# Block sums formed in PSUM, q weighted on GpSimd, and the last stores paired over two queues

## The chip, the core and the metric

The kernel runs on one core of a Trainium2 chip. Its engines work side by side: TensorE (PE in the profile; PEld is its weight load) multiplies matrices into the eight banks of PSUM, VectorE (DVE) and ScalarE (ACT) do elementwise work and read PSUM, GpSimd (POOL) does elementwise work in SBUF and issues loads, SyncE (SP) issues transfers. An engine runs its instructions in the order in which they were written, and waits on semaphores for the others. The metric is the device time of one execution in microseconds (us), as the median of several runs.

## The reference

Linear attention with cosine weights, followed by a gated feed-forward layer (SwiGLU). Cut to what is computed:

```python
# q, k, v: (8 batches, 8 heads, 576 positions, 64)
theta = np.pi / 2.0 * pos / S
def phi(x):                       # relu, then two weighted halves
    r = np.maximum(x, 0.0)
    return np.concatenate([r * cos(theta), r * sin(theta)], axis=-1)
q_p, k_p = phi(q), phi(k)
kv  = np.einsum('bhsf,bhsd->bhfd', k_p, v)
z   = np.sum(k_p, axis=2)
num = np.einsum('bhsf,bhfd->bhsd', q_p, kv)
den = np.einsum('bhsf,bhf->bhs', q_p, z)[..., None] + 1e-06
x   = (num / den).transpose(0, 2, 1, 3).reshape(4608, 512)
g   = x @ w_gate                  # 512 x 1536
out = (g / (1 + exp(-g)) * (x @ w_val)) @ w_out     # 1536 x 512
```

## The kernel before, in words

The 4608 tokens are cut into nine groups (tg 0 to 8) of 512 tokens, four tiles of 128 each. A group first runs twelve feed-forward steps (fc 0 to 11, `ffn_mm` L531): four matmuls with w_gate and four with w_val, each 512 columns wide; ACT takes silu of the first bank (L537), DVE multiplies it with the second into `ht` (L542). Then the group's output is made from `ht` and w_out.

For groups 0 and 1 that is done tile by tile (`ffn_out`, L580). For groups 2 to 8 `out_by_quarters` (L618) treats the product `ht` times w_out as a product of 2x2 blocks and computes it with seven block products in place of eight, each 12 matmuls of 256 columns (L640). The operands that this needs are sums of blocks: T1 to T4 of w_out are made once; S1 to S4 of `ht` are made in each group by DVE (`token_sum`, L611), the last parts of them behind the last feed-forward step (`sums_behind`). The products go, in this order, into PSUM banks: a (first product), e (S3 T3), b (S2 T2), a again (added to the first: this is C11), b again (S1 T1 added), c (A22 T4), b again (S4 B22 added). Each quarter C11, C12, C21, C22 of the output lies in an SBUF tile `ob`; every intermediate sum is made there. ACT copies bank a into C12 (L653); DVE's `added` (L647) then adds a bank, scaled by DOWN, to another quarter, five times a group: C22 = e + C12, C21 = b + C22, C22 = b + C22, C21 = c + C21, C12 = b + C12. ACT writes C11 (L663). A product that adds into b has to wait until DVE has read what stood there.

Attention is threaded between those steps. `at(slot, f)` puts a function into a plan, and `slot(n)` calls what is planned for step n of the whole program; a group has 16 slots, 12 for its feed-forward steps and four in `out_by_quarters` (`slot_of(0)` to `slot_of(3)`). For batch b of 2 to 7 there: POOL waits, by a tiny copy `hold2` (`load_behind`, L840), until the turned q of batch b-1 has landed, and then loads q, k and v of batch b (L107; k and v of batch 3 elsewhere). ACT takes relu of a quarter of q in place (L234) and DVE multiplies it with a table into `r_q` (`phi_q`, L251), four times a batch, in slots 11 to 14 of group b-2 for batches 4 and up. SP turns `r_q` by two DMA transposes into `phit` (L274) at the end of that group. k is treated by ACT and v by DVE (`vmul`, L255), and in the next group TensorE forms k times v (L301). `a_tile2` (L415) makes one tile of attention output, DVE divides it (L425, L434, L438) into `x`, and SP turns it by a DMA transpose into `xT` (L515) for the next group. SP also issues the stores of `ob` (L570), all in the order in which they are written.

`rel`, the pool of `r_q`, has one buffer; `raw`, that of q, k and v as loaded, three; `ob` two. PSUM banks are handed out by `take`, which picks the bank that has been unused for longest and avoids those held under a name (a, b, c, e above).

The profile calls each piece by the line of its instruction, or of the helper that issues it.

Of the kernel before, what the change touches and what calls it, by code (L numbers as in the profile page):

```python
# [11 lines left out]
BF16 = mybir.dt.bfloat16  # L12
FP16 = mybir.dt.float16
AF = mybir.ActivationFunctionType
ALU = mybir.AluOpType
# [3 lines left out]
def kernel(  # L19
# [10 lines left out]
    nc = tc.nc  # L30
    B, H, S, D = q.shape
    P = 128
    G = H // 2
    J = G // 2
    SH = 64
    NC = S // SH
    d_model, d_ff = moe_w_gate.shape
# [8 lines left out]
    UP = float(2 ** 12)  # L46
    DOWN = 1.0 / UP
    HC = FC // 2
    HT = T // 2
    HD = d_model // 2  # L50
# [3 lines left out]
    rel = ctx.enter_context(tc.tile_pool(name="rel", bufs=1))  # L54
# [13 lines left out]
    now = [0]  # L68
    held = {}

    def take(n, hold=None):

        taken = {x for r in held.values() for x in r}
        free = [b for b in range(0, 8, n) if not any(b <= x < b + n for x in taken)]

        b0 = min(free, key=lambda b: (n == 1 and hold is not None and hold[0] == "o" and b ^ 1 not in taken,
                                      sorted(used[b:b + n], reverse=True)))
        if hold is not None:
            held[hold] = range(b0, b0 + n)
        touch(range(b0, b0 + n))  # L80
        return banks[:, b0] if n == 1 else banks[:, b0:b0 + n]

    def touch(r):
        now[0] += 1
        for x in r:
            used[x] = now[0]
# [5 lines left out]
    raws = {}  # L92
# [102 lines left out]
    csk, cst = cs_all[:, 0], cs_all[:, 1]  # L195
# [49 lines left out]
    def phi_q(b, g):  # L245

        if g == 0:
            st[b, "q"] = rel.tile([P, G, NC, 2, D], BF16, name="r_q")
        o = raws[b, "q"][:, g]
        relu_op("act", o, o)  # L250
        nc.vector.tensor_tensor(out=st[b, "q"][:, g], in0=o.unsqueeze(2).to_broadcast([P, NC, 2, D]),  # L251
                                in1=tab, op=ALU.mult)

    def vmul(b, g):
        nc.vector.tensor_tensor(  # L255
# [262 lines left out]
    def ffn_mm(tg, fc, lo=0, hi=GH, which=(0, 1)):  # L518

        n = (hi - lo) * SH  # L520
        ts = slice(lo // 2, hi // 2)
        fs = slice(fc * P, (fc + 1) * P)
        if 0 in which:
            if 2 * n <= 512:
                both = take(1, ("f", tg, fc, lo))
                st["f", tg, fc, lo] = [both[:, 0:n], both[:, n:2 * n]]
            else:
                st["f", tg, fc, lo] = [take(1)[:, 0:n] for _ in range(2)]
        for i in which:
            for kc in range(KC):  # L530
                nc.tensor.matmul(out=st["f", tg, fc, lo][i], lhsT=(wg_sb, wv_sb)[i][:, kc, fs], rhs=xT[tg][:, ts, kc],  # L531
                                 start=(kc == 0), stop=(kc == KC - 1))
# [34 lines left out]
    def store(t, cols=slice(0, d_model), queues=None):  # L567
        for e in range(2):
            idx = 2 * t + e
            (queues or (nc.sync, nc.sync))[e].dma_start(out=out_v[idx // NC, idx % NC][:, cols],  # L570
                                                        in_=ob_of(t)[e * SH:(e + 1) * SH, cols])

    def ffn_out(t, f0=0, f1=None):

        f1 = FC if f1 is None else f1
        if f0 == 0:
            o_ps[t] = take(1, ("o", t))
        r = t % OUT * P
        for fc in range(f0, f1):
            nc.tensor.matmul(out=o_ps[t], lhsT=ht[:, fc, r:r + P], rhs=wo_sb[:, fc],  # L580
                             start=(fc == 0), stop=(fc == FC - 1))
        if f1 < FC:
            return
        ps = o_ps.pop(t)
        give_back(("o", t))
        if t % 2 == 0:
            nc.scalar.mul(out=ob_of(t), in_=ps, mul=DOWN)
        else:
            nc.vector.tensor_single_scalar(out=ob_of(t), in_=ps, scalar=DOWN, op=ALU.mult)
        store(t)  # L590
# [21 lines left out]

    def sums_behind(fc):
        for n, lo, hi in {7: ((3, 0, 4),), 8: ((1, 0, 4),), 9: ((2, 0, 4),), 10: ((4, 0, 4), (3, 4, 6)),
                          11: ((1, 4, 6), (2, 4, 6), (4, 4, 6))}.get(fc, ()):
            token_sum(n, lo, hi)

    def out_by_quarters(tg, slot_of):  # L618

        last = tg == NTG - 1  # L620
        t0 = tg * OUT
        for t in (t0, t0 + 2):
            ob_of(t)
        C11, C12 = (obs[t0 // 2][:, :, x * HD:(x + 1) * HD] for x in range(2))
        C21, C22 = (obs[t0 // 2 + 1][:, :, x * HD:(x + 1) * HD] for x in range(2))

        def home(nm, parts=1):
            return [take(1, ("o", tg, nm, i)).rearrange("p (t x) -> p t x", x=HD) for i in range(parts)]

        def free(nm, parts=1):  # L630
            for i in range(parts):
                give_back(("o", tg, nm, i))

        def at_of(x, i):
            return x[i][:, 0] if len(x) == 2 else x[0][:, i]

        def product(to, a, b, first):
            for i in range(2):
                for kc in range(HC):
                    nc.tensor.matmul(out=at_of(to, i), lhsT=a[:, kc, i * P:(i + 1) * P], rhs=b[:, kc],  # L640
                                     start=first and kc == 0 and (i == 0 or len(to) == 2),
                                     stop=kc == HC - 1, skip_group_check=True)

        def added(o, ps, x):
            for i in range(len(ps)):
                sl = slice(i, i + 1) if len(ps) == 2 else slice(0, 2)
                nc.vector.scalar_tensor_tensor(out=o[:, sl], in0=ps[i][:, 0:1] if len(ps) == 2 else ps[i],  # L647
                                               scalar=DOWN, in1=x[:, sl], op0=ALU.mult, op1=ALU.add)

        nb = 2 if last else 1  # L650
        a = home("a")
        product(a, aq[:, 0, 0], bq[:, 0, 0], True)
        nc.scalar.mul(out=C12, in_=a[0], mul=DOWN)  # L653
        e = home("e")
        product(e, S3, T3, True)
        added(C22, e, C12)
        b = home("b", nb)
        free("e")
        slot_of(0)
        product(b, S2, T2, True)  # L660
        added(C21, b, C22)
        product(a, aq[:, 1, 0], bq[:, 1, 0], False)
        nc.scalar.mul(out=C11, in_=a[0], mul=DOWN)  # L663
        free("a")
        if last:
            for t in (t0, t0 + 1):
                store(t, slice(0, HD))
        slot_of(1)
        product(b, S1, T1, False)
        added(C22, b, C22)  # L670
        if last:
            for t in (t0 + 2, t0 + 3):
                store(t, slice(HD, d_model))
        c = home("c")
        product(c, aq[:, 1, 1], T4, True)
        added(C21, c, C21)
        free("c")
        for t in (t0 + 2, t0 + 3):
            store(t, slice(0, HD) if last else slice(0, d_model))
        slot_of(2)  # L680
        product(b, S4, bq[:, 1, 1], False)
        added(C12, b, C12)
        free("b", nb)
        for t in (t0, t0 + 1):
            store(t, slice(HD, d_model) if last else slice(0, d_model), (nc.sync, nc.scalar) if last else None)
        slot_of(3)


# [149 lines left out]
    def load_behind(b):  # L838

        nc.gpsimd.tensor_copy(out=hold2, in_=phit[b - 1][0:1, :, 0, 0, 0])  # L840
        load(b, "q")
        if b > 3:
            load_kv(b)

    def load_kv(b):
        for nm in ("k", "v"):
            load(b, nm)
# [7 lines left out]
    for b in range(2, B):  # L855
        s0 = SLOTS * (b - 1)
        keng = "dve" if b == 2 else "act"
        steps = [lambda b=b, g=g: phi_q(b, g) for g in range(G)]
        steps += [lambda b=b, g=g: (relu_k(b, g, g + 1, keng), vmul(b, g)) for g in range(G)]
        if b == 2:  # L860
            fs, tq = [s0 + i for i in (0, 0, 1, 1, 4, 5, 5, 6)], (s0 + 2, s0 + 2)
        else:
            p0 = s0 - SLOTS
            fs, tq = [p0 + 11 + i for i in range(8)], (p0 + 15, p0 + 16)
            if b == 3:
                fs, tq = [p0 + 12 + i for i in range(4)] + [s0 + 4, s0 + 4, s0 + 5, s0 + 5], (s0 + 2, s0 + 2)
            at(p0 + 3 if b < 5 else p0 + 1, lambda b=b: load_behind(b))
        tk = (s0 + 4, s0 + {2: 8, 3: 7}.get(b, 5))
        for s, f in zip(fs, steps):
            at(s, f)  # L870
        for e in range(2):
            at(tq[e], lambda b=b, e=e: qturn_dma(b, e))
        at(tk[-1], lambda b=b: kv_mm(b), lambda b=b: kv_out2(b))
        at(tk[-1] + 1, lambda b=b: kv_free(b))
# [59 lines left out]
```

## Time and profile before

| what | us |
|---|---|
| median of 8 runs (323.44 to 324.16) | 323.8 |
| the profiled execution itself | 323.11 |
| its span, first to last instruction | 321.0 |
| DVE busy in it | 225.0 |
| POOL busy in it | 35.3 |
| the seven-product stretch of group 7 (274.06 to 283.1) | 9.04 |
| the same stretch of group 2 (110.9 to 121.04) | 10.14 |

Times of single instructions come from one execution, the one of 323.11 us. In a row of a timeline the first number is the start in us from the beginning of the span, the second the length; an `x` with a number counts instructions that were merged. In brackets stands how long the engine sat idle before it, and what it waited for. TensorE's ends are modelled, and spans on POOL are rough. Groups follow each other at about 32.8 us: group 2 begins at 87.8, group 3 at 121.3, group 4 at 154.1, group 5 at 187.0, group 6 at 219.9, group 7 at 252.3 and group 8 at 283.2.

### The profile page before, as it was taken

Reading aid. Unit: us, or ns where it says so; the run is one execution under the profiler, and the core shown is the slowest. Engines: PE = TensorE matmul, PEld = TensorE weight load, DVE = VectorE, ACT = ScalarE, POOL = GpSimd, SP = SyncE. Lnnn points to the kernel's source line nnn. Section 1 sums busy time; section 2 is a strip of 40 time slices with the busy share of each in tenths; the row PEclk is TensorE's granted clock in tenths of the full one; section 3 lists DMA queues with packets and bytes.
Section 4 is the critical chain, followed back from the end, with each engine's and each line's share of the span. In section 5 each row is a group of like instructions: output and inputs, shape, how many; then the busy total and the mean of one; then the engine's idle time right before and its main releaser. Section 6 shows DMA issues by size and latency. Waiting matters only on the chain.

```text
span 321.0 us, 6625 instructions
## 1 busy us (share of the span) xinstructions
PE 308.9 (96%) x2624; PEld 182.8 (57%) x2624; DVE 225.0 (70%) x448; ACT 130.1 (41%) x237; POOL 35.3 (11%) x60
## 2 busy tenths in 40 slices
PE   8899999999999989999999999999999999999990
PEld 4596555454445575558554855476547644854580
DVE  7873876788658888598859875988487448643750
ACT  7553556662436345334433543244431132223210
POOL 6755102010100200020002000300000000000000
PEclk9999999999999999999999999999999999999997
DMA  7999999988996987999696969597941411150014
GB/s 260 216 199 197 205 203 142 217 112 109 175 196 89 162 110 153 128 144 146 141 136 87 205 133 131 76 184 158 139 67 33 99 34 34 35 130 3 0 27 104
DMA packets 74862, 41.06 MB, mean 128 GB/s; under 512 B 50000, under 2 KB 69968, under 8 KB 74832
## 3 DMA queue, kind: packets, MB, share of 16 engines
q1 hardware_dynamic: 52480, 22.95, 40.1%
q0 software_dynamic: 22192, 17.57, 36.5%
q8 instruction: 20, 0.33, 0.4%
q10 hardware_dynamic: 160, 0.13, 0.2%
q14 instruction: 10, 0.08, 0.1%
HBM read 37.75 MB, written 9.44 MB: 147 GB/s over the span
## 4 chain that ended last, share of the span: by engine, by line
PE 76%; DVE 10%; DMA 5%; issue 3%; SPq 2%; ACT 2%; DVEq 0%; POOLq 0%; POOL 0%; ACTq 0%
PE banks L531 49%; PE banks L640 14%; PE banks L580 6%; DMA phit<-r_q 3%; PE banks L301 2%; DMA raw_q<-in_q_dram 2%; DVE ht L542 2%; DVE ob L647 2%; DVE sums L611 2%; PE banks L415 1%; SPq L274 1%; DVE r_q L251 1%; PE banks L461 1%; PE banks L397 1%; SPq L570 1%
## 5 line engine op out<-in xcount | busy, mean ns | idle before, releaser
L537 ACT ACTIVATE sg<-banks 128x512 bf16<-128x512 f32 (+2 forms) x116 | 65.8, 568 | 120.2 <-PE banks L531 113.2
L531 PE MATMUL banks<-xT,wv_sb 128*128 128x512 bf16 (+2 forms) x464 | 111.3, 364 | 0.0
L531 PE MATMUL banks<-xT,wg_sb 128*128 128x512 bf16 (+2 forms) x464 | 111.3, 364 | 0.0
L542 DVE TENSOR_TENSOR ht<-sg,banks 128x512 f16<-128x512 bf16 (+2 forms) x116 | 74.5, 648 | 51.5 <-PE banks L531 44.5
L531 PEld LDWEIGHTS <-wv_sb 128*128 128x128 bf16 x464 | 44.9, 98 | 48.7
L531 PEld LDWEIGHTS <-wg_sb 128*128 128x128 bf16 x464 | 43.2, 98 | 41.5
L640 PEld LDWEIGHTS <-ht 128*128 128x128 f16 x336 | 32.4, 98 | 6.8 <-issue 2.9
L647 DVE SCALAR_TENSOR_TENSOR ob<-banks,ob 128x512 f32<-128x512 f32 (+1 forms) x38 | 24.6, 647 | 13.7 <-PE banks L640 13.5
L640 PEld LDWEIGHTS <-sums 128*128 128x128 f16 x252 | 24.6, 98 | 2.9
L255 DVE TENSOR_TENSOR v<-raw_v,tab 128x1152 bf16<-128x1152 bf16 x31 | 22.7, 752 | 0.2 <-ACT raw_v L691 0.2
L580 PE MATMUL banks<-wo_sb,ht 128*128 128x512 f16 x96 | 22.7, 379 | 0.0
L438 DVE TENSOR_TENSOR x<-banks,rec 128x512 bf16<-128x512 f32 (+1 forms) x32 | 21.6, 675 | 1.3 <-PE banks L397 0.3
L640 PE MATMUL banks<-wt_sb,ht 128*128 128x256 f16 x168 | 19.5, 272 | 2.2 <-DVE ob L647 2.2
L251 DVE TENSOR_TENSOR r_q<-raw_q,tab 128x1152 bf16<-128x1152 bf16 x24 | 17.9, 752 | 5.2 <-ACT raw_q L234 5.1
L640 PE MATMUL banks<-wo_sb,ht 128*128 128x256 f16 x168 | 20.6, 273 | 0.0
L640 PE MATMUL banks<-wt_sb,sums 128*128 128x256 f16 x168 | 19.5, 273 | 0.0
L234 ACT ACTIVATE raw_k<-raw_k 128x576 bf16<-128x576 bf16 (+1 forms) x25 | 17.0, 694 | 0.0
L234 ACT ACTIVATE raw_q<-raw_q 128x576 bf16<-128x576 bf16 x24 | 15.4, 675 | 2.9 <-DMA raw_q<-in_q_dram 2.9
L611 DVE TENSOR_TENSOR sums<-ht 128x1024 f16<-128x1024 f16 (+1 forms) x28 | 15.5, 553 | 0.2
L840 POOL COPY hold<-phit 1x2 bf16<-1x2 bf16 x5 | 0.9, 175 | 132.2 <-DMA phit<-r_q 132.2
L580 PEld LDWEIGHTS <-ht 128*128 128x128 f16 x96 | 9.1, 98 | 8.9 <-issue 0.2
L415 PEld LDWEIGHTS <-phit 128*128 128x128 bf16 (+1 forms) x240 | 10.0, 100 | 6.5 <-issue 1.3
(95 smaller groups left out, 210.4 us busy)
## 6 DMA issues: line engine op xcount, KB each, us to landing
out_dram<-ob SPq DMA_DIRECT2D x64, 128.0 KB, 2.4
raw_k<-in_k_dram POOLq DMA_DIRECT2D x7, 576.0 KB, 8.8
raw_q<-in_q_dram POOLq DMA_DIRECT2D x6, 576.0 KB, 6.5
raw_v<-in_v_dram POOLq DMA_DIRECT2D x6, 576.0 KB, 11.6
wo_sb<-in_moe_w_out_dram POOLq DMA_DIRECT2D x3, 512.0 KB, 13.1
wg_sb<-in_moe_w_gate_dram POOLq DMA_DIRECT2D x5, 256.0 KB, 8.9
wv_sb<-in_moe_w_val_dram POOLq DMA_DIRECT2D x5, 256.0 KB, 9.2
wo_sb<-in_v_dram SPq DMA_DIRECT2D x2, 576.0 KB, 4.1
```

The source lines that it names most:

```text
L234: nc.scalar.activation(out=out, in_=in_, func=AF.Relu)
L251: nc.vector.tensor_tensor(out=st[b, "q"][:, g], in0=o.unsqueeze(2).to_broadcast([P, NC, 2, D]), in1=tab, op=ALU.mult)
L255: nc.vector.tensor_tensor(out=v2s[b % 2][:, g, :, :, 0:D], in0=(first if b == 0 and g == 0 else {"v": raw_of(b, "v")})["v"][:, g].unsqueez ...
L415: nc.tensor.matmul(out=ps[ms, e, g * D1:(g + 1) * D1], lhsT=phit[b][:, e, g, c:c + n].rearrange("p c s -> p (c s)"), rhs=kv2s[b % 2][:, e, ...
L438: nc.vector.tensor_tensor(out=st["x", t].rearrange("p (y e d) -> p e y d", e=2, d=D)[:, :, ys], in0=ps[:, :, 0:2 * J * D1].rearrange("p e ...
L531: nc.tensor.matmul(out=st["f", tg, fc, lo][i], lhsT=(wg_sb, wv_sb)[i][:, kc, fs], rhs=xT[tg][:, ts, kc], start=(kc == 0), stop=(kc == KC - 1))
L537: nc.scalar.activation(out=sg[:, 0:n], in_=st["f", tg, fc, lo][0], func=AF.Silu, scale=DOWN)
L542: nc.vector.tensor_tensor(out=ht[:, fc, r:r + n], in0=st.pop(("s", tg, fc, lo))[:, 0:n], in1=ps[1], op=ALU.mult)
L580: nc.tensor.matmul(out=o_ps[t], lhsT=ht[:, fc, r:r + P], rhs=wo_sb[:, fc], start=(fc == 0), stop=(fc == FC - 1))
L611: nc.vector.tensor_tensor(out=o[:, lo:hi], in0=x[:, lo:hi], in1=y[:, lo:hi], op=op)
L640: nc.tensor.matmul(out=at_of(to, i), lhsT=a[:, kc, i * P:(i + 1) * P], rhs=b[:, kc], start=first and kc == 0 and (i == 0 or len(to) == 2), ...
L647: nc.vector.scalar_tensor_tensor(out=o[:, sl], in0=ps[i][:, 0:1] if len(ps) == 2 else ps[i], scalar=DOWN, in1=x[:, sl], op0=ALU.mult, op1= ...
```

## The change

Three things are done at once.

`out_by_quarters` forms sums in PSUM. ACT copies bank a into bank b before the third product, which then adds to it. DVE adds the scaled C22, which ACT has written from e, to bank b, and puts the result into bank c; the sixth product adds to that. C21 and C12 become plain scaled copies, of bank c by ACT and of bank b by DVE. The bank manager `take` learns which banks were last filled whole by matmuls (`filled`), so that a bank which another engine writes first (`seeded`) is one of these. Four banks are held at once now, a, b, e and c.

The part S4(4,6) of the sums is made after DVE's reading of bank b, and no longer in `sums_behind`. For batches 4 to 7 `phi_q` on ACT and DVE is replaced by `phi_q_whole` on POOL: 18 operations of 128x256, called right behind that batch's loads. Batches 2 and 3 keep `phi_q`.

In the last group, C11, C22 and C21 are each stored by two transfers of two tiles (`store_two`), one on SP and one on ACT, in place of four on SP. C12 is stored as before.

```diff
-    def take(n, hold=None):
+    filled = [False] * 8
+
+    def take(n, hold=None, fills=False, seeded=False):
 
         taken = {x for r in held.values() for x in r}
-        free = [b for b in range(0, 8, n) if not any(b <= x < b + n for x in taken)]
+        free = [b for b in range(0, 8, n) if not any(b <= x < b + n for x in taken)
+                and (filled[b] or not seeded)]
...
+        filled[b0:b0 + n] = [fills or seeded] * n
...
+    def phi_q_whole(b):
+        r_q = st[b, "q"] = rel.tile([P, G, NC, 2, D], BF16, name="r_q")
+        for c in range(NC):
+            for w in range(2):
+                nc.gpsimd.tensor_scalar(out=r_q[:, :, c, w], in0=raws[b, "q"][:, :, c], scalar1=0.0,
+                                        scalar2=csk[:, c, w:w + 1], op0=ALU.max, op1=ALU.mult)
...
+    def store_two(t, cols):
+        for e in range(2):
+            (b, c), (b1, _) = divmod(2 * t + e, NC), divmod(2 * t + 2 + e, NC)
+            assert b == b1
+            (nc.sync, nc.scalar)[e].dma_start(
+                out=out_v[b, c:c + 3:2, :, cols].rearrange("c p f -> p c f"),
+                in_=obs[t // 2][e * SH:(e + 1) * SH, :, cols])
...
         for n, lo, hi in {7: ((3, 0, 4),), 8: ((1, 0, 4),), 9: ((2, 0, 4),), 10: ((4, 0, 4), (3, 4, 6)),
-                          11: ((1, 4, 6), (2, 4, 6), (4, 4, 6))}.get(fc, ()):
+                          11: ((1, 4, 6), (2, 4, 6))}.get(fc, ()):
...
+        def copied(eng, o, ps, x=DOWN):
+            for p_, o_ in each(ps, o):
+                if eng == "act":
+                    nc.scalar.mul(out=o_, in_=p_, mul=x)
+                else:
+                    nc.vector.tensor_single_scalar(out=o_, in_=p_, scalar=x, op=ALU.mult)
...
-        a = home("a")
+        a = home("a", fills=True)
         product(a, aq[:, 0, 0], bq[:, 0, 0], True)
-        nc.scalar.mul(out=C12, in_=a[0], mul=DOWN)
-        e = home("e")
+        b = home("b", nb, seeded=True)
+        for p_, o_ in each(b, a[0]):
+            nc.scalar.copy(out=p_, in_=o_)
+        e = home("e", fills=True)
         product(e, S3, T3, True)
-        added(C22, e, C12)
-        b = home("b", nb)
+        nc.scalar.mul(out=C22, in_=e[0], mul=DOWN)
+        c = home("c", seeded=True)
         free("e")
+        product(b, S2, T2, False)
+        for p_, o_, x_ in each(b, c[0], C22):
+            nc.vector.scalar_tensor_tensor(out=o_, in0=x_, scalar=UP, in1=p_, op0=ALU.mult, op1=ALU.add)
+        token_sum(4, 4, 6)
         slot_of(0)
-        product(b, S2, T2, True)
-        added(C21, b, C22)
         product(a, aq[:, 1, 0], bq[:, 1, 0], False)
-        nc.scalar.mul(out=C11, in_=a[0], mul=DOWN)
+        copied("act", C11, a)
         free("a")
         if last:
-            for t in (t0, t0 + 1):
-                store(t, slice(0, HD))
+            store_two(t0, slice(0, HD))
         slot_of(1)
         product(b, S1, T1, False)
-        added(C22, b, C22)
+        for p_, x_ in each(b, C22):
+            nc.vector.scalar_tensor_tensor(out=x_, in0=p_, scalar=DOWN, in1=x_, op0=ALU.mult, op1=ALU.add)
         if last:
+            store_two(t0 + 2, slice(HD, d_model))
+        product(c, aq[:, 1, 1], T4, False)
+        copied("act", C21, c)
+        free("c")
+        if last:
+            store_two(t0 + 2, slice(0, HD))
+        else:
             for t in (t0 + 2, t0 + 3):
-                store(t, slice(HD, d_model))
-        c = home("c")
-        product(c, aq[:, 1, 1], T4, True)
-        added(C21, c, C21)
-        free("c")
-        for t in (t0 + 2, t0 + 3):
-            store(t, slice(0, HD) if last else slice(0, d_model))
+                store(t)
         slot_of(2)
         product(b, S4, bq[:, 1, 1], False)
-        added(C12, b, C12)
+        copied("dve", C12, b)
         free("b", nb)
...
         load(b, "q")
         if b > 3:
             load_kv(b)
+            phi_q_whole(b)
...
-        steps = [lambda b=b, g=g: phi_q(b, g) for g in range(G)]
+        steps = [lambda b=b, g=g: phi_q(b, g) for g in range(G)] if b < 4 else [lambda: None] * G
```

The helper `each` walks over a sum's one or two banks (the last group gives b two). The remaining lines of the diff pass `fills=True` where matmuls fill a bank whole.

More of the change, by code (lines that the diff above doesn't have):

```diff
@@ L527, in ffn_mm @@
             else:
-                st["f", tg, fc, lo] = [take(1)[:, 0:n] for _ in range(2)]
+                st["f", tg, fc, lo] = [take(1, fills=n == 512)[:, 0:n] for _ in range(2)]
         for i in which:
@@ L576, in ffn_out @@
         if f0 == 0:
-            o_ps[t] = take(1, ("o", t))
+            o_ps[t] = take(1, ("o", t), fills=True)
         r = t % OUT * P
@@ L625, in out_by_quarters, with home @@
         C21, C22 = (obs[t0 // 2 + 1][:, :, x * HD:(x + 1) * HD] for x in range(2))
-        def home(nm, parts=1):
-            return [take(1, ("o", tg, nm, i)).rearrange("p (t x) -> p t x", x=HD) for i in range(parts)]
+        def home(nm, parts=1, **kw):
+            return [take(1, ("o", tg, nm, i), **kw).rearrange("p (t x) -> p t x", x=HD) for i in range(parts)]
         def free(nm, parts=1):
@@ L632, in free @@
                 give_back(("o", tg, nm, i))
-        def at_of(x, i):
-            return x[i][:, 0] if len(x) == 2 else x[0][:, i]
         def product(to, a, b, first):
@@ L639, in product, with each @@
                 for kc in range(HC):
-                    nc.tensor.matmul(out=at_of(to, i), lhsT=a[:, kc, i * P:(i + 1) * P], rhs=b[:, kc],
-                                     start=first and kc == 0 and (i == 0 or len(to) == 2),
+                    nc.tensor.matmul(out=to[i][:, 0] if len(to) == 2 else to[0][:, i],
+                                     lhsT=a[:, kc, i * P:(i + 1) * P], rhs=b[:, kc],
+                                     start=first and kc == 0 and i == 0,
                                      stop=kc == HC - 1, skip_group_check=True)
[L644 to L648, printed above, removed]
+        def each(ps, *others):
+            if len(ps) == 1:
+                return [(ps[0], *others)]
+            return [(ps[i][:, 0:1], *(o[:, i:i + 1] for o in others)) for i in range(2)]
@@ L680, in out_by_quarters @@
         slot_of(2)
         product(b, S4, bq[:, 1, 1], False)
-        added(C12, b, C12)
+        copied("dve", C12, b)
         free("b", nb)
         for t in (t0, t0 + 1):
-            store(t, slice(HD, d_model) if last else slice(0, d_model), (nc.sync, nc.scalar) if last else None)
+            store(t, *((slice(HD, d_model), (nc.sync, nc.scalar)) if last else ()))
         slot_of(3)
@@ L863 @@
             p0 = s0 - SLOTS
-            fs, tq = [p0 + 11 + i for i in range(8)], (p0 + 15, p0 + 16)
+            fs, tq = [p0 + 12, p0 + 12] + [p0 + 11 + i for i in range(2, 8)], (p0 + 15, p0 + 16)
             if b == 3:
```

## The prediction

> **What bounds the kernel now.** I read the page first for the bound, then PE's waits for what is left between its instructions, then the timeline around the largest wait, then the timeline of the end, and last the POOL and SP rows, because the change gives POOL new work.
>
> From the page (part 1 and a row of part 5) and from the table of waits:
>
> ```profile
> PE 308.9 (96%) x2624; PEld 182.8 (57%) x2624; DVE 225.0 (70%) x448; ACT 130.1 (41%) x237; POOL 35.3 (11%) x60
> L640 PE MATMUL banks<-wt_sb,ht 128*128 128x256 f16 x168 | 19.5, 272 | 2.2 <-DVE ob L647 2.2
> ```
>
> ```profile
> PE banks L640 <- DVE ob L647: 2.2, 4, 0.9
> ```
>
> TensorE is the bound: between its start and the last product it has only this one recurring wait, four times, 2.2 us in all. Where it sits, in the timeline of group 2 (start us, duration us, engine, line):
>
> ```profile
> 114.83 1.47 PE L640 MATMUL banks<-wo_sb,ht 128*128 128x256 f16 x12
> 115.22 0.68 DVE L647 SCALAR_TENSOR_TENSOR ob<-banks,ob 128x512 f32<-128x512 f32 x1
> 115.81 0.75 DVE L251 TENSOR_TENSOR r_q<-raw_q,tab 128x1152 bf16<-128x1152 bf16 x1
> 116.48 0.68 DVE L647 SCALAR_TENSOR_TENSOR ob<-banks,ob 128x512 f32<-128x512 f32 x1
> 117.22 2.78 PE L640 MATMUL banks<-wt_sb,ht 128*128 128x256 f16 x24 [0.92 <-DVE ob L647]
> ```
>
> The fifth product (117.22) adds into the bank that the second L647 (C21, 116.48) reads. DVE reached it late because two r_q weightings (L251) and the sum S4 stood ahead of it. The same wait is 0.39, 0.30 and 0.57 us in groups 3, 4 and 5, and absent in 6, 7 and 8, where no r_q is made.
>
> The end, in the timeline:
>
> ```profile
> 309.85 4.31 SPq L570 DMA_DIRECT2D out_dram<-ob  x7
> 313.00 1.43 ACTq L570 DMA_DIRECT2D out_dram<-ob  x2
> 313.16 0.42 DVE L647 SCALAR_TENSOR_TENSOR ob<-banks,ob 128x256 f32<-128x256 f32 x1 [0.23 <-PE banks L640]
> ```
>
> Arithmetic ends at 313.58, the span at 321.0. SP issues 14 stores from 309.85 for 8.79 us, 0.63 each, so until 318.64; the last lands and the program closes 2.36 us later. SP's issuing is the end, not the bytes.
>
> POOL and the transposes of q for the last batch, from the timelines of SP, POOL and all engines:
>
> ```profile
> 191.46 8.44 SPq L274 DMA_TRANSPOSE phit<-r_q  x2
> 224.38 8.19 SPq L274 DMA_TRANSPOSE phit<-r_q  x2
> ```
>
> ```profile
> 204.16 0.18 POOL L840 COPY hold<-phit 1x2 bf16<-1x2 bf16 x1 [30.36 <-DMA phit<-r_q]
> 204.67 0.74 POOL L107 DMA_DIRECT2D raw_q<-in_q_dram  x1 [0.34 <-PE banks L531]
> ```
>
> ```profile
> 211.35 0.68 ACT L234 ACTIVATE raw_q<-raw_q 128x576 bf16<-128x576 bf16 x1 [1.80 <-DMA raw_q<-in_q_dram]
> ```
>
> This is a loop over batches: transposes of b-1 are issued, land 12.7 us later, release POOL's hold, the load of q(b) lands 7.2 us after that, r_q(b) is made, and SP transposes it at 224.38. Between landing and transposing there are 13.0 us.
>
> **What the Trainium skill says.** "SBUF — State Buffer", Who interferes with whom: a VectorE instruction with two SBUF inputs contends with a GpSimd instruction that reads SBUF; whichever starts first holds the shared pair for its whole length. The trace shows a hint of such a lock, of another form of operation, at the start:
>
> ```profile
> 0.94 0.59 POOL L150 IOTA wt_sb<- 128x512 f32 x1
> 1.11 0.59 DVE L186 COPY posk<-pos 64x9 f32<-64x9 f32 x1
> 1.48 0.19 POOL masks.py:197 MEMSET ident<- 128x128 bf16 x1
> 1.72 0.17 DVE L187 TENSOR_SCALAR posk<-pos 64x9 f32<-64x9 f32 x1
> ```
>
> A nine-element copy took 0.59 us and ended with POOL's second operation; its neighbour took 0.17. "GPSIMD Engine Reference", Elementwise: 1.03 cycles an element at 1.2 GHz for small bodies, about 1.8 for longer ones. MEMSETs here agree with the low end: 530 ns for 520 columns, 194 for 128, hence 0.86 ns a column plus 84 ns. "PSUM — Partial Sum Buffer", The four PSUM rules: writes of VectorE and ScalarE leave the accumulate bits alone, so a matmul without start adds to what they wrote where an earlier matmul left the bit set. That is what `filled` and `seeded` in take() arrange; no run here shows it yet. "DMA: Bandwidth & Descriptors", Issuing engines are not separate DMA queues: a second issuing engine saves issue time alone, which is what the trace says is short at the end.
>
> **The change, part by part.**
>
> 1. Sums in PSUM. TensorE has the same 84 products a group, so nothing is gained on it directly. DVE loses two of five L647 (0.69 each); ACT gets a copy of bank a into bank b, and writes C22 and C21: two more operations of about 0.60 (rows L653, L663) in each of 7 groups. New waits, each with its cover. (a) The third product waits for ACT's copy: bank a is full near 112.35, the copy would take L653's place (112.41 to 113.01), and product e covers it until 113.5: margin 0.5. ACT has nothing queued ahead then. (b) The fifth product waits until DVE has read b into c (0.69). Bank b ends near 115.0, the read would run 115.05 to 115.75, and the fourth product covers until 116.13: margin 0.35. Group 7, which has no L251, shows precisely this wait met today: 278.03 to 278.72 before the product at 279.14. A DVE write to PSUM from a PSUM read is not in the trace: I take L647's 0.69, ends 0.6 and 0.9; only above 1.0 does it cost. (c) C22 is needed at 115.05; ACT has it at about 114.35. (d) C12 and C21 become plain copies; as long as L647, nothing. Cost 0.
>
> 2. S4(4,6) behind that read, and r_q off DVE and ACT for batches 4 to 7. Per group DVE loses 4 x 0.752 us and ACT 4 x 0.675. Both are off the path except at the wait above: minus 0.92+0.39+0.30+0.57 = **-2.18 us**. What is next late there is (b), with its 0.35 spare.
>
> 3. r_q on POOL: 18 TENSOR_SCALARs of 128x256 a batch, queued behind three loads and ahead of the next hold, which waits for these very values' transposes anyway. Price of one: low end 0.86 ns x 256 + 100 = 0.32 us; 1.8 cycles an element plus 0.18 gives 0.56; 0.9 if scalars fetched per instruction come on top. I take **0.45**, 8.1 us a batch, against 13.0 free (15.3 for batch 4): hidden; without that cover, each us is paid. SP's transposes therefore go out when they do now. Beside DVE: S1(4,6) and S2(4,6) (0.42 each, two SBUF inputs) must be done when the third product reaches its fifth matmul, near 113.93; S2 ends at 113.14 now, 0.8 spare. If every such DVE operation waits for one POOL operation at most, they lose 0.2 to 0.45 each, in batch 4's window also the two sums ahead. I put **+0.4 us** for all groups (ends 0 and 1).
>
> 4. The last stores. SP issues 5 and ACT 5 instead of 14 and 2. The three paired ones are released at 309.83, 310.96 and about 312.45 (ACT's C21). ACT: third issue 312.5 to 313.2, then two for C12 until 313.9 and 314.6 (0.67 each). SP is done by 314.3. Issuing more rows is not dearer: SP's loads of 256 rows at the start took 0.45. So 314.6 + 2.36 = 316.96, a gain of 4.0; since 0.75 MB (twelve 64 KB quarters) now leave within some 4 us, and the busiest microsecond of the tail moved 202 GB/s, I hold back 0.3: **-3.7 us** (ends -2.5 and -4.1).
>
> Sum on the profiled execution: 321.0 - 2.18 + 0.4 - 3.7 = 315.5 span; 2.1 lie around it (323.11 - 321.0), so 317.6. The median of runs is 0.7 above that execution, hence **318.3 us**; the case's own range is 317.0 to 319.5. About 0.2% (0.65 us) is what a measurement can tell from no change.
>
> **Rivals.**
> - The lock lets DVE in only when POOL's 18 operations are over. They wait for nothing between them, and the copy at 1.11 ended not with IOTA (1.53) but with the MEMSET behind it (1.67). Place: S1 and S2 in front of the third product. With POOL running 110.5 to 118.6, 144.0 to 152.1 and 178.2 to 186.3, S2 ends 0.9 later (in batch 6's group 0.5, S1 being through) and misses its need at 113.93, 147.2 and 180.2 by 5.5, 5.8 and 6.6 us, S4 by about 1.1 in batch 7's group: +19.0 us on a sum without the 0.4, 337 us. It decides once S1 and S2 together wait about 2.6 us in each of three groups (0.8 spare plus a third of the 5.5 gained), six POOL operations; below that the change stays faster. Against it: one sample of another form, and spans on POOL are rough.
> - POOL is too slow. Above 0.7 us an operation the loop of transposes, load and weighting exceeds a group's 32.8 us; lateness grows by batch, and SP's in-order queue holds up the xT transposes behind. At 1.0 us the loop slips some 4.4 us a batch, 17 by batch 7, of which about 4 are slack (SP is free for 1.7 us before that group's xT transposes start at 234.32; they end at 247.14, land 3.0 later, and are needed at 252.31): +13 us, 331 us. Even with before: near 0.9. Same evidence against: 0.29 us for a 128x128 select that reads and writes.
> - The stall only changes its name: (a) or (b) is late, the 2.2 us stay: 320.5 us. Against: margins of 0.5 and 0.35.
> - The tail stays: stores are limited by moving and landing, gain 1.5: 320.5 us. Against: landing is a steady 1.9 to 2.3.
>
> **How the numbers follow.** Forecast 0.60; stall renamed 0.09; tail stays 0.06; no change, by a half-held lock, 0.03; lock held 0.15; POOL too slow 0.07. Faster 0.75, same 0.03, slower 0.22. The range 316.8 to 325.0 takes in the small rivals and leaves out about 0.04 below and 0.16 above.
>
> **What will show it.** Right: no PE wait at the products line over 0.1 us; the last store issue within 1.2 us of DVE's end; 18 POOL operations of 0.3 to 0.6 us ending before SP's transposes. Wrong: sums (now 0.42 and 0.68) that take microseconds, PE waiting for them; POOL operations of 0.8 us or more and SP waiting for r_q.

## The result and the profile after

The changed kernel takes 340.9 us (337.83 to 342.14) where the kernel before, on the same chip, takes 323.9. The ratio is 1.0515, with a 95% interval of 1.0495 to 1.0535: 5% slower. The forecast was 318.3 us, with a range up to 325.0.

The profiled execution took 340.08 us, its span 338.3. From the page, part 1 (busy us, share of the span, instructions), the chain that ended last by engine, and one row of part 5 (busy, mean ns of one | idle before, releaser):

```profile
PE 314.9 (93%) x2624; PEld 185.3 (55%) x2624; DVE 206.3 (61%) x418; ACT 129.2 (38%) x236; POOL 122.1 (36%) x132
...
PE 48%; POOL 25%; DMA 16%; SPq 4%; DVE 2%; ACT 2%; issue 1%; POOLq 0%; ACTq 0%
...
L262 POOL TENSOR_SCALAR r_q<-raw_q,cs_all 128x256 bf16<-128x256 bf16 x72 | 86.1, 1209 | 17.7 <-DMA raw_q<-in_q_dram 13.0
```

TensorE issues the same 2624 matmuls, but it is no longer the one bound. A quarter of the chain now runs through POOL. Before, it read:

```profile
PE 76%; DVE 10%; DMA 5%; issue 3%; SPq 2%; ACT 2%; DVEq 0%; POOLq 0%; POOL 0%; ACTq 0%
```

The row of part 5 names the reason: one weighting of 128x256 takes 1.2 us, not the 0.45 us that the forecast put in.

What TensorE waits for, from the table of its waits (total us, times, longest us):

```profile
PE banks L426 <- DMA phit<-r_q: 11.8, 6, 4.2
PE banks L542 <- DMA xT<-x: 3.9, 3, 2.4
PE banks L383 <- DVE qf L375: 1.5, 1, 1.5
```

The first is the turned q, which comes late; the second is the turned `x` of the next group, whose transposes stand behind those of q in SP's queue. The wait of the fifth product for DVE (2.2 us before) is gone. So part 2 of the change did what it should, and something else took more.

How the lateness runs, first in POOL's timeline around batch 6 (start, length, instruction, in brackets the idle time before it and what ended that):

```profile
220.54 0.47 POOL L868 COPY hold<-phit 1x2 bf16<-1x2 bf16 x1 [10.88 <-DMA phit<-r_q]
...
228.08 21.51 POOL L262 TENSOR_SCALAR r_q<-raw_q,cs_all 128x256 bf16<-128x256 bf16 x18 [4.79 <-DMA raw_q<-in_q_dram]
```

then in SP's timeline:

```profile
131.30 9.10 SPq L285 DMA_TRANSPOSE phit<-r_q  x2
...
170.17 8.05 SPq L285 DMA_TRANSPOSE phit<-r_q  x2
...
209.69 8.06 SPq L285 DMA_TRANSPOSE phit<-r_q  x2
217.85 6.75 SPq L526 DMA_TRANSPOSE xT<-x  x4
...
249.62 9.10 SPq L285 DMA_TRANSPOSE phit<-r_q  x2
```

Read it as a ring. Transposes start at 209.69, and land 10.85 us later, when POOL's hold goes (220.54). The loads that it issues let the weighting start 7.54 us after that (228.08). The weighting and the step to SP take 21.54 us, and the next transposes start at 249.62. Together 39.93 us, while a group took 32.8 before. The ring had 13.0 us for the weighting and now has to hold 21.5. Each turn comes later against the groups, and the groups themselves are stretched by waiting: the four starts are 38.9, 39.5 and 39.9 us apart.

The new wait costs more than its own length. TensorE's timeline at the longest one, with a shorter wait before and one after it:

```profile
142.27 0.30 PE L426 MATMUL banks<-kv,phit 128*128 128x65 bf16 x4 [2.81 <-DMA phit<-r_q]
142.41 1.03 PE L542 MATMUL banks<-xT,wg_sb 128*128 128x512 bf16 x4
...
181.16 0.42 PE L426 MATMUL banks<-kv,phit 128*64 128x65 bf16 x7 [4.22 <-DMA phit<-r_q]
181.52 1.89 PE L542 MATMUL banks<-xT,wg_sb 128*128 128x512 bf16 x4
...
184.76 1.03 PE L542 MATMUL banks<-xT,wg_sb 128*128 128x512 bf16 x4
...
232.35 1.84 PE L542 MATMUL banks<-xT,wg_sb 128*128 128x512 bf16 x4 [2.43 <-DMA xT<-x]
```

Four matmuls of one kind take 1.89 us right after the longest wait and 1.03 us three microseconds later. The view by windows of the stretch around the longest wait (window, its length, PE busy and matmuls, granted clock, DMA share, GB/s):

```profile
181.00:182.00 1.00, 0.84 (x9) 0.60 0.33 63
182.00:183.00 1.00, 1.00 (x4) 0.50 0.41 79
183.00:184.00 1.00, 1.00 (x3) 0.50 0.72 29
184.00:185.00 1.00, 1.00 (x5) 0.69 0.92 141
185.00:186.00 1.00, 1.00 (x6) 1.00 1.14 167
```

The granted clock is at half for about 3 us. The Trainium skill, "TensorE: Matmul & The Clock Gate", section "What's actually happening", describes a gate that passes all or half of the clock's pulses, according to how busy TensorE was in a window of about 3.4 us; it puts the half rate after an idle window of that length. This trace agrees on the two rates (0.50, then 1.00), but not on the length: half clock followed waits of 4.22, 2.43 (at 232.35) and 2.68 us (at 260.55), two of them shorter than the window, and did not follow one of 2.81 us (at 142.27). So the length of a wait alone does not decide; what else does is not shown here. Summed in the same view, the missing share of the clock over the three stretches is 1.7 + 1.7 + 3.0 = 6.4 us.

Now the span, 321.0 to 338.3, is accounted for. PE's busy time grew by 6.0 (308.9 to 314.9), about the half-clock stretches. Its idle time grew by 11.3 (12.1 to 23.4): 11.8 + 3.9 of new waits, 1.2 at the start (`qf`), less 2.2 at the fifth product and less 3.4 at the end.

The end itself, in the timeline of all engines:

```profile
330.52 3.21 SPq L588 DMA_DIRECT2D out_dram<-ob  x3
...
333.82 1.50 ACTq L581 DMA_DIRECT2D out_dram<-ob  x2
333.83 0.42 DVE L671 TENSOR_SCALAR ob<-banks 128x256 f32<-128x256 f32 x1 [0.23 <-PE banks L656]
333.83 1.19 SPq L581 DMA_DIRECT2D out_dram<-ob  x2
```

DVE's last copy ends at 334.25, the last issue at 335.32, the span at 338.3: 4.05 us behind the arithmetic, where it was 7.42.

### The profile page after: what moved, and what is told of

It reads as the page before. It is cut to its first block, busy times and chain, and to the rows that moved or that the text cites. A ratio compares the mean times of both kernels' runs of the same rounds, so it can differ in the third digit from the quotient of the medians.

```text
span 338.3 us, 6645 instructions
## 1 busy us (share of the span) xinstructions
PE 314.9 (93%) x2624; PEld 185.3 (55%) x2624; DVE 206.3 (61%) x418; ACT 129.2 (38%) x236; POOL 122.1 (36%) x132
## 4 chain that ended last, share of the span: by engine, by line
PE 48%; POOL 25%; DMA 16%; SPq 4%; DVE 2%; ACT 2%; issue 1%; POOLq 0%; ACTq 0%
PE banks L542 28%; POOL r_q L262 25%; PE banks L656 9%; DMA phit<-r_q 9%; DMA raw_q<-in_q_dram 8%; PE banks L599 6%; SPq L285 4%; PE banks L426 1%; PE banks L312 1%; PE banks L472 1%; PE banks L408 1%; DVE v L266 1%; PE banks L172 1%; PE banks L352 0%; PE banks L514 0%
## 5 line engine op out<-in xcount | busy, mean ns | idle before, releaser
L542 PE MATMUL banks<-xT,wg_sb 128*128 128x512 bf16 (+2 forms) x464 | 113.0, 369 | 3.9 <-DMA xT<-x 3.9
L542 PE MATMUL banks<-xT,wv_sb 128*128 128x512 bf16 (+2 forms) x464 | 112.9, 368 | 0.0
L262 POOL TENSOR_SCALAR r_q<-raw_q,cs_all 128x256 bf16<-128x256 bf16 x72 | 86.1, 1209 | 17.7 <-DMA raw_q<-in_q_dram 13.0
L542 PEld LDWEIGHTS <-wv_sb 128*128 128x128 bf16 x464 | 45.3, 99 | 50.0 <-issue 2.2
L542 PEld LDWEIGHTS <-wg_sb 128*128 128x128 bf16 x464 | 43.3, 99 | 47.3 <-issue 5.0
L656 PEld LDWEIGHTS <-ht 128*128 128x128 f16 x336 | 33.0, 100 | 4.5
L656 PEld LDWEIGHTS <-sums 128*128 128x128 f16 x252 | 25.5, 101 | 3.7
L426 PE MATMUL banks<-kv,phit 128*128 128x65 bf16 (+1 forms) x240 | 13.0, 198 | 11.8 <-DMA phit<-r_q 11.8
L656 PE MATMUL banks<-wo_sb,ht 128*128 128x256 f16 x168 | 21.9, 283 | 0.0
L426 PEld LDWEIGHTS <-phit 128*128 128x128 bf16 (+1 forms) x240 | 10.6, 103 | 19.0 <-DMA phit<-r_q 12.7
L656 PE MATMUL banks<-wt_sb,sums 128*128 128x256 f16 x168 | 21.0, 285 | 0.0
L669 ACT ACTIVATE ob<-banks 128x512 f32<-128x512 f32 x14 | 8.4, 597 | 28.5 <-PE banks L656 26.5
L686 DVE SCALAR_TENSOR_TENSOR banks<-ob,banks 128x512 f32<-128x512 f32 (+1 forms) x8 | 5.0, 630 | 15.6 <-PE banks L656 15.6
## 6 DMA issues: line engine op xcount, KB each, us to landing
raw_v<-in_v_dram POOLq DMA_DIRECT2D x6, 576.0 KB, 11.9
```

What stands on the lines that cost most here:

```text
L262: nc.gpsimd.tensor_scalar(out=r_q[:, :, c, w], in0=raws[b, "q"][:, :, c], scalar1=0.0, scalar2=csk[:, c, w:w + 1], op0=ALU.max, op1=ALU.mult)
L426: nc.tensor.matmul(out=ps[ms, e, g * D1:(g + 1) * D1], lhsT=phit[b][:, e, g, c:c + n].rearrange("p c s -> p (c s)"), rhs=kv2s[b % 2][:, e, ...
L656: nc.tensor.matmul(out=to[i][:, 0] if len(to) == 2 else to[0][:, i], lhsT=a[:, kc, i * P:(i + 1) * P], rhs=b[:, kc], start=first and kc == ...
```

## The experiments

Nine kernels were run, each beside the kernel before on the same chip. Where no number of runs is given, time and ratio come from several runs.

**The weighting back on ACT and DVE.** All else of the change stays.

```diff
-            phi_q_whole(b)
...
-        steps = [lambda b=b, g=g: phi_q(b, g) for g in range(G)] if b < 4 else [lambda: None] * G
+        steps = [lambda b=b, g=g: phi_q(b, g) for g in range(G)]
```

> The changed kernel with q of batches 4 to 7 weighted by ACT and DVE again, in the slots behind the reading of bank b. Theory A (all of the loss is POOL's weighting, which takes 1.13 us an operation): the other parts keep their gains of 2.2 us (the wait at the fifth product) and 3.4 us (the tail, 4.05 us behind DVE's last operation in place of 7.42), so about 318.3 us, no wait at the products above 0.1 us, and a granted clock back at 0.99. Theory B (forming the sums in PSUM brings waits or slower products of its own): clearly above 320 us, with waits at the products' line or products that are slower than before.

Measured: 318.6 us (317.92 to 318.98), ratio 0.9829 (0.9806 to 0.9853). From its page and, second, its timeline at the fifth product of group 2:

```profile
PE 309.3 (98%) x2624; PEld 182.7 (58%) x2624; DVE 215.6 (68%) x434; ACT 138.2 (44%) x252; POOL 35.1 (11%) x60
```

```profile
115.11 0.70 DVE L686 SCALAR_TENSOR_TENSOR banks<-ob,banks 128x512 f32<-128x512 f32 x1 [0.94 <-PE banks L656]
115.72 0.42 DVE L630 TENSOR_TENSOR sums<-ht,sums 128x512 f16<-128x512 f16 x1
116.05 2.25 DVE L255 TENSOR_TENSOR r_q<-raw_q,tab 128x1152 bf16<-128x1152 bf16 x3
116.14 2.78 PE L656 MATMUL banks<-wt_sb,ht 128*128 128x256 f16 x24
```

The whole loss goes with this one edit, and the mean granted clock is 0.999 (0.980 in the changed kernel; the 0.993 of the kernel before was lost behind its last product). DVE reads bank b at 115.11, ahead of the sum and of three weightings, and is through at 115.81; the fifth product follows the fourth at 116.14 with no wait in brackets. So the sums in PSUM do no harm, and with them in place it is enough to put the sum and the weightings behind this read: they need not leave DVE for the stall to go. The new order without the sums in PSUM was not run, so what those sums themselves bring stays open.

What puts the weightings behind the read is in the change, but was not named with it above. `slot_of(0)` is now called after the read, and one further line of the diff plans the first two steps of `phi_q`, for batches 4 to 7, both in that slot, where they stood in slots 11 and 12:

```diff
-            fs, tq = [p0 + 11 + i for i in range(8)], (p0 + 15, p0 + 16)
+            fs, tq = [p0 + 12, p0 + 12] + [p0 + 11 + i for i in range(2, 8)], (p0 + 15, p0 + 16)
```

In the changed kernel these steps are empty for the four batches; here, and in the versions of the changed kernel below that leave weightings on ACT and DVE, the line takes effect. In the execution shown, TensorE also waits once, 1.2 us, for `xT` at the start of group 5 (186.80), which the profile before does not have. The kernel with the stores alone, whose groups up to the last are those of before, has such a wait too (0.8 us), so it is not a mark of the new order.

**The weighting on POOL alone**, in the kernel before.

```diff
+            phi_q_whole(b)
...
+        steps = [lambda b=b, g=g: phi_q(b, g) for g in range(G)] if b < 4 else [lambda: None] * G
```

> The kernel before with POOL's weighting of q alone added. Theory A: the same loop of transposes, load and weighting bounds it, so it loses what the changed kernel loses against the one without POOL, some 22 us: about 344 us (346 if the 2.2 us wait at the fifth product stays although DVE has no weighting there). Theory B: the loss belongs to the PSUM sums, so this one is within some 5 us of 323.9.

Measured: 343.3 us, ratio 1.0589 (1.0556 to 1.0621). Its table of TensorE's waits begins:

```profile
PE banks L422 <- DMA phit<-r_q: 12.8, 6, 4.0
PE banks L538 <- DMA xT<-x: 4.4, 3, 2.7
```

These are the waits of the changed kernel (there at L426 and L542). The move to POOL brings them without any other part. The stall at the fifth product is gone here as well, since DVE no longer makes the weightings; so the parts do not add: +5.9% here already holds that gain, and the stores take 1.0% off, which leaves 4.9% beside the 5.15% measured, within the two intervals.

**The stores alone**, in the kernel before.

```diff
-            for t in (t0, t0 + 1):
-                store(t, slice(0, HD))
+            store_two(t0, slice(0, HD))
```

and likewise for C22 and C21 of the last group.

> The kernel before with the paired stores of the last group alone. Issue theory: SP's 14 issues in a row are the tail, so it ends 3.4 us earlier as in the changed kernel, about 320.5 us. Rival (moving and landing the bytes are the tail): within 1 us of 323.9.

Measured: 320.6 us, ratio 0.9901 (0.9875 to 0.9927). The end in its timeline:

```profile
311.34 3.31 SPq L577 DMA_DIRECT2D out_dram<-ob  x3
...
314.75 1.20 SPq L570 DMA_DIRECT2D out_dram<-ob  x2
314.79 1.45 ACTq L570 DMA_DIRECT2D out_dram<-ob  x2
```

SP issues five stores where it issued fourteen, and both queues are done by 316.24; the span is 319.3, so what is left behind the last issue is 3.1 us, 0.7 more than before the change. The part of the tail that was SP's issuing goes.

**The order and PSUM alone**: the first experiment with the old stores in the last group.

```diff
-            store_two(t0, slice(0, HD))
+            for t in (t0, t0 + 1):
+                store(t, slice(0, HD))
```

> As e1, but with the stores of before. It keeps the gain of the order and of the PSUM sums alone. Theory A: 2.2 us below 323.9, about 321.7, and 3.4 us above e1. Theory B: at or above 323.9.

Measured: 322.2 us, ratio 0.9947 (0.9933 to 0.996), which is 1.7 us less than before, and 3.6 above the version with the new stores.

**The price of a POOL operation, three ways.** First each operation cut into two of 128 columns:

```diff
-                nc.gpsimd.tensor_scalar(out=r_q[:, :, c, w], in0=raws[b, "q"][:, :, c], scalar1=0.0,
-                                        scalar2=csk[:, c, w:w + 1], op0=ALU.max, op1=ALU.mult)
+                for gs in (slice(0, 2), slice(2, 4)):
+                    nc.gpsimd.tensor_scalar(out=r_q[:, gs, c, w], in0=raws[b, "q"][:, gs, c], scalar1=0.0,
+                                            scalar2=csk[:, c, w:w + 1], op0=ALU.max, op1=ALU.mult)
```

> The changed kernel with every POOL operation of 128x256 cut into two of 128x128, the same columns in all. If the 1.13 us is per column (4.4 ns each), one takes about 0.57 to 0.65 and the run of a batch 20 to 24 us, and the time is 341 to 348. If it is a fixed cost per operation, one still takes near 1.0 us, the run near 38 us, and the loop loses some 17 us more for each of the batches 5 to 7: about 395.

Then the scalar per partition replaced by a constant, so that q is weighted by 0.5 throughout:

```diff
-                                        scalar2=csk[:, c, w:w + 1], op0=ALU.max, op1=ALU.mult)
+                                        scalar2=0.5, op0=ALU.max, op1=ALU.mult)
```

> The changed kernel with the constant 0.5 in place of the per-partition cosine and sine as POOL's second scalar, so q of batches 4 to 7 is weighted wrongly. If fetching the scalar of each partition is what costs, an operation falls to about 0.5 us, a run to 9 us, and the time to about 318.6. If it is the body (two operations an element, bf16 in and out), it stays near 1.1 us and the time near 341.

And the multiplication left out, so that `r_q` is relu of q without weights:

```diff
-                nc.gpsimd.tensor_scalar(out=r_q[:, :, c, w], in0=raws[b, "q"][:, :, c], scalar1=0.0,
-                                        scalar2=csk[:, c, w:w + 1], op0=ALU.max, op1=ALU.mult)
+                nc.gpsimd.tensor_single_scalar(out=r_q[:, :, c, w], in_=raws[b, "q"][:, :, c], scalar=0.0,
+                                               op=ALU.max)
```

> The changed kernel with POOL taking the maximum with 0 alone, so q of batches 4 to 7 is not weighted by cosine and sine. Two sizes gave 0.71 us for 128 columns and 1.13 for 256: 0.29 fixed and 3.3 ns a column. If the two operations an element make the slope, it falls to a half or less, so an operation takes 0.5 to 0.7 us, a run 9 to 13 us, which fits into the 13.0 free, and the time is about 318.6. If conversion from and to bf16 or the walk over the pattern makes it, an operation stays at 1.0 us or more and the time at 328 or more.

The view of the tile `r_q` gives the time of one operation (ns, least/median/most; first and last start in us). In the changed kernel:

```profile
L262 POOL TENSOR_SCALAR r_q<-raw_q,cs_all x72: 1128/1134/1743, 109.1 to 248.5; 128x256 bf16<-128x256 bf16 x72
```

in the halved one:

```profile
L263 POOL TENSOR_SCALAR r_q<-raw_q,cs_all x144: 704/714/1362, 109.0 to 270.3; 128x128 bf16<-128x128 bf16 x144
```

with the constant:

```profile
L262 POOL TENSOR_SCALAR r_q<-raw_q x72: 1054/1059/1493, 109.2 to 241.6; 128x256 bf16<-128x256 bf16 x72
```

and with max alone:

```profile
L262 POOL TENSOR_SCALAR r_q<-raw_q x72: 833/838/1442, 109.5 to 226.5; 128x256 bf16<-128x256 bf16 x72
```

From 256 and 128 columns: 1134 - 714 = 420 ns for 128 columns, 3.28 ns a column, and 294 ns fixed. Neither of the two pure cases held for the halved kernel: it took 360.1 us (one run), since 36 operations carry 36 fixed parts. The scalar that is fetched per partition costs 75 ns, where the forecast's upper end had put in 340 ns (0.9 against 0.56 us); the second arithmetic step costs 221 ns; what is left is the body. The kernels took 331.5 us with the constant and 319.7 with max alone (one run each). With max alone, price and time both lie between their two cases. With the constant, the price stayed near its second case (1.06 us), but the time fell well below it: a batch took 19.3 us in place of 21.5, and the ring passes that on several times.

**Fewer operations on POOL.** Of the nine token slots (the loop over `NC` in `phi_q_whole`), POOL weights the first PC (2 x PC operations a batch), and ACT and DVE the others in the slots where they did so before.

```diff
+    PC = 5
+    def phi_q_part(b):
...
-        for c in range(NC):
+        for c in range(PC):
...
-        o = raws[b, "q"][:, g]
+        o = raws[b, "q"][:, g, lo:]
```

> POOL weights 5 of the 9 position slots of q (10 operations), ACT and DVE the other four as in e1. Loop theory: 10 x 1.16 = 11.6 us fit into the 13.0 us between landing and transposing, so POOL costs nothing: within 1 us of 318.6. Rival (POOL's work costs in proportion, by sharing the port with DVE or by delaying what it sits between): 10/18 of 22 us, about 331.

Measured: 318.3 us (317.67 to 318.35), ratio 0.9824 (0.9802 to 0.9845). POOL's timeline around batch 6:

```profile
208.60 11.78 POOL L265 TENSOR_SCALAR r_q<-raw_q,cs_all 128x256 bf16<-128x256 bf16 x10 [3.79 <-DVE sums L633]
```

and SP's:

```profile
217.33 4.96 SPq L584 DMA_DIRECT2D out_dram<-ob  x8
222.40 8.03 SPq L288 DMA_TRANSPOSE phit<-r_q  x2
```

POOL is through at 220.38, while SP still issues the group's stores until 222.29; the transposes follow these at once, as in the kernel before (there 224.38). Twelve microseconds of POOL are free. They ran beside the sums of DVE, and no product waited for a sum, which also answers the rival of the lock.

With PC = 7:

> As e7 with 7 of 9 slots on POOL (14 operations, 16.2 us). Loop theory: transposes to landing 12.5, load 7.2, POOL 16.2, 0.2 for issue make 36.1 us against a group's 32.4; batch 4 is 0.9 late, then 3.7 more each, 12 by batch 7, of which 4 are slack: about 326.6 (323 to 329). Rival (in proportion, 14/18 of 22 us): about 335.7.

Measured: 325.9 us (323.37 to 327.08), ratio 1.0051 (1.0031 to 1.0071). POOL's runs take 16.0 to 17.4 us, and SP's transposes start 36.5, 34.8 and 33.6 us apart: the ring is just longer than a group.

All versions that keep the rest of the change, by POOL's time per batch:

| version | POOL, us a batch | time, us |
|---|---|---|
| none on POOL | 0 | 318.6 |
| 10 of 18 operations | 11.9 | 318.3 |
| 18, max alone | 15.5 | 319.7 |
| 14 of 18 operations | 16.9 | 325.9 |
| 18, constant | 19.3 | 331.5 |
| the change | 21.5 | 340.9 |
| 36 halves | 27.1 | 360.1 |

The version with max alone, the one with the constant and the halves are single runs. The time is flat at 11.9 us, inside the 13.0 of room, is about 1 us higher at 15.5, and then rises by some 3.5 us for each us of POOL, (340.9 - 319.7) / (21.5 - 15.5), about as many as batches go around it (four). The first two versions, at 1.7% below the kernel before, beat both kernels, and cannot be told apart.

## Why the prediction was wrong

The step that failed is one term in part 3: "Price of one ... I take 0.45, 8.1 us a batch, against 13.0 free: hidden". One operation took 1.13 us (the median; 1.21 in the mean) and a batch 21.5 us (20.9 to 22.2). Even the upper end, 0.9, was too low. It was put together from POOL's MEMSETs (0.86 ns a column), one 128x128 select of 0.29 us, and the Trainium skill, "GPSIMD Engine Reference", Elementwise. The 1.03 to 1.8 cycles an element there (the page gives 1.8 as a best case), at 1.2 GHz and read as a column of all partitions, are 0.86 to 1.5 ns; the same section's 2.6 cycles for two-input operations, which the forecast left aside, are 2.2. Measured were 3.28 ns a column, 3.9 such cycles. The section has no figure for this operation, and these, carried over to it, are too low; the trace decides. None of the rows used was an operation of two arithmetic steps on bf16 read from SBUF.

- What the forecast said of the free time held. It put 13.0 us beside the weighting; 11.9 us on POOL cost nothing and 16.9 cost about 7 us.
- The rival that came true is "POOL is too slow", held at 0.07. Its mechanism is what the traces show: the ring of transposes, load and weighting longer than a group, and lateness that grows by batch until TensorE waits for `phit`, with the transposes of `x` held up behind in SP's queue. Its 331 us was worked out for 1.0 us an operation, and without the half clock after the waits. It was near: 325.9 us were measured at 16.9 us a batch (0.94 for each of 18) and 331.5 at 19.3 (1.07).
- The rival of the lock named 337 us, nearer to the result, by another mechanism, and that one fell: TensorE never waited for a sum. DVE's timeline of the changed kernel, beside POOL's first run (109.05 to 131.27):

```profile
112.30 0.42 DVE L630 TENSOR_TENSOR ht<-ht 128x512 f16<-128x512 f16 x1
112.76 0.65 DVE L630 TENSOR_TENSOR sums<-ht 128x512 f16<-128x512 f16 x1
```

The second sum took 0.65 us in place of 0.43, and the first nothing more than before. The Trainium skill, "SBUF — State Buffer", Who interferes with whom, calls the pair of ports that DVE and POOL share an exclusive lock. The trace shows less: the second sum ran from 112.76 to 113.41, inside one POOL operation that the profile puts at 112.66 to 113.80. As far as POOL's rough spans can tell, DVE was slowed by 0.22 us, and was shut out neither until that operation ended nor for the whole run. Of the +0.4 us put in for this, nothing is seen in the version with PC = 5.

- Part 1, cost 0, was right. The waits (a) and (b) stayed away, with (b) where it was worked out: DVE's read ran 115.14 to 115.84 in the changed kernel (forecast 115.05 to 115.75), and the product started at 116.18, with no wait (forecast 116.13). DVE's write to PSUM took 0.70 us (0.69 taken).
- Part 2, -2.18 us, was right in kind: the waits are gone from the table, and the fourth experiment, with part 1, gained 1.7. That it needed POOL was not so.
- Part 4, -3.7 us, was right in kind and 0.1 to 0.5 too large: -3.4 in the trace, 1.0% or 3.2 us alone, 3.6 between the fourth experiment and the first. What follows the last issue is 3.0 to 3.1 us and not 2.36.
- The sum apart from POOL's price was near: 318.3 us forecast, 318.6 measured with no weighting on POOL. In part that is luck: the -2.18 came out 0.5 smaller, and of the +0.4 nothing was seen, and the two errors cancel. The forecast was lost on one price, and with a chance of 0.07 on the case in which that price is wrong, although no row of the profile had shown the operation.

## What to carry to other kernels

Before work is moved to an engine that looks idle, take the price from an operation of the same kind there (same operands, types and number of arithmetic steps), and if no row has one, run that operation once by itself or give the case in which it is several times dearer a real chance. Compare it with the free time of the ring that it joins (what it waits for, up to what waits for it), not with the share in which the engine is idle: POOL was busy for 11% of the span, and had room for 12 us a batch. When a queue in order hands on the result, what stands behind it is late as well, and a part of the moved work often fits where the whole doesn't.

## What the runs showed of the hardware

- A POOL TENSOR_SCALAR on bf16 costs 0.29 us and 3.28 ns a column, from two sizes; of the 1.13 us for 256 columns, the second arithmetic step is 0.22 us and the scalar per partition 0.08 us. DVE makes the same product of 1152 columns in 0.75 us (behind ACT's relu), where POOL needs 1.13 us for 256.
- Waits of a few microseconds are dearer on TensorE than they look: after three of them the granted clock stood at half for 3 to 6 us, and the same 2624 matmuls were busy for 309.3 us (mean clock 0.999, no weighting on POOL), 314.9 (0.980, the change) and 319.2 (0.946, halves). A wait of 2.43 us was enough in one place, and one of 2.81 was not in another. That is seen in the traces; no run held the clock apart from the waits.
- A DVE sum with two inputs in SBUF ran to its end inside a POOL operation that reads SBUF, in 0.65 us in place of 0.43, as far as POOL's rough spans can tell.
